# A gated linear-attention and adapter kernel: one decay array per chunk, work moved between engines, and an order written out by hand

## The chip, the cores and the metric

The kernel runs on one core of a Trainium2 chip. The time is device time in microseconds (us), from a launch of the whole program; "before" was run three times. The core has five engines that each work through their own queue in order: TensorE (PE in the profile; PEld is its weight load), VectorE (DVE), ScalarE (ACT), GpSimd (POOL) and SyncE (SP), which here only issues transfers. They meet through semaphores. SBUF is the working memory of 128 partitions; PSUM, in eight banks, receives TensorE's results.

## The reference

There are 4 batches, 8 heads, 768 tokens and 48 dimensions per head. Each head carries a 48 x 48 state:

```
cur   = (u * k_t) outer v_t
y_t   = r_t @ (state + cur)
state = w_t[:, None] * state + k_t outer v_t
```

The 8 heads of a token make a row x of 384. An adapter follows, with 8 experts of rank 16, of which the two with the largest logit are used:

```
logits = x @ w_gate
w      = softmax over the two largest logits
out    = x + sum over those two e of  w_e * (x @ A[e]) @ B[e]
```

## The kernel before

Tokens are cut into chunks of 128; 6 chunks make one batch's sequence, 24 chunks (t = 0 to 23) the whole. A tile of r and k (`rk`, loaded by SP into a ring of 10, 512 KB with padding at first, 384 KB in two transfers later) has the head dimensions of two heads on its 128 partitions, so 4 pairs x 128 tokens are 512 elements for r and as many for k.

Inside a chunk the recurrence is written as matrix products, with decays as exponentials of summed logarithms. For each chunk:

- `ln` (L174, ScalarE) takes the logarithm of w, two chunks at a time.
- `cs` (L186, L189, TensorE) sums it over tokens by a matmul with a triangle. The triangle is 256 wide: its first half gives the sum before a token, for r; its second half the negative sum up to a token, for k. The result `cs_ps` has 1,024 elements and fills two PSUM banks. Two chunks make a frame (FRAME = 2): in the second chunk of a frame, another matmul with `ones` (L189) adds the whole of the first.
- `exps` (L202, ScalarE) exponentiates all of it in place, and `mult` (L211, VectorE) multiplies r and k by it in one instruction: `rkd`.
- `amm` (L255, TensorE) multiplies the decayed k by the decayed r, per head: scores `a_ps` in two banks. `aev` (L261, VectorE) masks them: `at`.
- `qmul` (L206, GpSimd) is r times k; `dgmm` (L229, TensorE) sums it with u: 8 numbers per token. `dgev` (L241, VectorE) copies these out of PSUM, and `dv` (L246, GpSimd) multiplies v by them.
- `ktr` (L224, TensorE) transposes k, `ktev` (L236, VectorE) copies it to `ks`, and `kv` (L271, TensorE) adds k outer v to the state `s_ps`, which lives in PSUM. `resc` (L276, VectorE) multiplies the state by the frame's decay, once per frame (8 times); `sev` (L282, ScalarE) copies it to `sb`.
- `ymm` (L289, L296, L301, TensorE) adds three parts into `y_ps`: dv, the old state times r, and `at` times v. `yev` (L307, ScalarE) copies it to `xT`.

The adapter works on groups of three chunks (the last two groups have two and one). `zl` (L325, TensorE) makes logits and x @ A in `z_ps`; `top`, `gsel`, `gnorm` (VectorE), `gexp` (ScalarE), `gmul`, `gmul2` (GpSimd) make the weights; `zw` (L391, VectorE) multiplies them in; `zT` (L402, TensorE) transposes, `zTev` (L410, VectorE) copies. Per chunk then `dmm` (L418, L420, TensorE) makes x plus the adapter's part in `d_ps`, `oev` (L425, ScalarE) copies it to `res` and `store` (L429, SP) sends it out. `z_ps`, `zT_ps` and `d_ps` share the tag "m" and with it a single PSUM bank.

The eight banks: `cs_ps` 2, `a_ps` 2, `kd` (for `ktr` and `dgmm`) 1, `s_ps` 1, `y_ps` 1, "m" 1.

Order: every stage has a number in `OFFSET`; stage f of chunk t is put at t + OFFSET[f], and the instructions are issued in that order (a late stage of an adapter group is moved back by up to two chunks). As each engine works in order, this list sets what stands behind what in every queue, SP's loads and stores among them. `consts` (L152 to L162) loads u, then the adapter's two weight arrays, and casts each on GpSimd right after its load.

Of the kernel before, what the change touches and what calls it, by code (L numbers as in the profile page):

```python
# [18 lines left out]
L = 128  # L19
NC = S // L  # L20
# [6 lines left out]
FRAME = 2  # L27
# [3 lines left out]
OFFSET = dict(  # L31
    load_w=-9.0,
    load_rk=-8.5,
    load_v=-8.0,
    ln=-3.0,
    cs=-2.6,
    decay=-2.45,
    exps=-2.4,
    qmul=-2.2,
    mult=-1.9,  # L40
    dgmm=-1.3,
    dgev=-1.1,
    dv=-0.9,
    amm=-1.25,
    aev=-0.8,
    ktr=-1.2,
    ktev=-1.0,
    kv=-0.5,
    resc=-0.3,
    sev=-0.2,  # L50
    ymm=0.2,
    yev=0.5,
    zl=1.0,
    top=1.1,
    gexp=1.2,
    gsel=1.25,
    gmul=1.3,
    gnorm=1.4,
    gmul2=1.5,
    zw=1.6,  # L60
    zT=1.7,
    zTev=1.8,
    dmm=2.0,
    oev=2.2,
    store=2.4,
)
# [3 lines left out]
def tile_kernel(ctx: ExitStack, tc: tile.TileContext, rk, w, v, ublk, aw, bm, out):  # L70
# [82 lines left out]
    def consts(t):  # L153
        if t == 0:
            nc.sync.dma_start(out=ub_f, in_=ublk)
            nc.gpsimd.tensor_copy(out=ub, in_=ub_f)
        if t == 1:
            nc.sync.dma_start(out=aw_f, in_=aw)
            nc.gpsimd.tensor_copy(out=aw_b, in_=aw_f)
        if t == 2:  # L160
            nc.sync.dma_start(out=b_f, in_=bm)
            nc.gpsimd.tensor_copy(out=b_b, in_=b_f)  # L162

    def ln(t):
        w_in, i = wseq[t]
        if t < 2:
            n = 1
        elif t % FRAME == 0:
            n = FRAME
        else:  # L170
            return
        lw = lws[(t // FRAME) % NLW]
        o = t % FRAME
        nc.scalar.activation(out=lw[:, o:o + n, :, 0:D].rearrange("p c h d -> p (c h) d"),  # L174
                             in_=w_in[:, 0:n].rearrange("p c (h d) -> p (c h) d", h=H), func=ACT.Ln)

    def lwof(t, p):
        lw = lws[(t // FRAME) % NLW]
        return lw[:, t % FRAME, 2 * p:2 * p + 2, :].rearrange("p a b -> p (a b)")

    def cs(t):
        cs_ps = pp.tile([128, P, 2, L], F32, name="cs_ps")
        for p in range(P):
            o = cs_ps[:, p].rearrange("p a b -> p (a b)")
            odd = t % FRAME
            nc.tensor.matmul(o, lhsT=lwof(t, p), rhs=tri.rearrange("p a b -> p (a b)"),  # L186
                             start=(p % 2 == 0), stop=not odd, skip_group_check=True)
            if odd:
                nc.tensor.matmul(o, lhsT=lwof(t - 1, p), rhs=ones.rearrange("p a b -> p (a b)"),  # L189
                                 start=False, stop=True, skip_group_check=True)  # L190
        st[t]["cs"] = cs_ps

    def decay(t):
        c = t % NC
# [4 lines left out]

    def exps(t):  # L200
        c_ = st[t]["cs"].rearrange("p a s b -> p (a s b)")
        nc.scalar.activation(out=c_, in_=c_, func=ACT.Exp)  # L202
# [6 lines left out]
    def mult(t):  # L209
        rkd = wk.tile([128, 2, P, L], BF16, name="rkd", bufs=3)  # L210
        nc.vector.tensor_mul(rkd, st[t]["rk"], st[t]["cs"].rearrange("p a s b -> p s a b"))  # L211
        st[t]["rkd"] = rkd
# [6 lines left out]
    def ktr(t):  # L219
        if t % NC == NC - 1:  # L220
            return
        kT = bank(t)[:, 0:256].bitcast(BF16).rearrange("p (a b) -> p a b", a=P)
        for p in range(P):
            nc.tensor.transpose(kT[:, p, :], st[t]["rkd"][:, 1, p, :], ident)  # L224
# [6 lines left out]
    def ktev(t):  # L231
# [4 lines left out]
        nc.vector.tensor_copy(out=ks, in_=kT[:, :, 0:D])  # L236
        st[t]["ks"] = ks

    def dgev(t):
        dg = wk.tile([128, H, 1], F32, name="dg")  # L240
        nc.vector.tensor_copy(out=dg.rearrange("p a b -> p (a b)"), in_=st[t]["kd"][:, 256:256 + H])  # L241
        st[t]["dg"] = dg

    def dv(t):
        o = dvs[t % NDV]
        nc.gpsimd.tensor_mul(o[:, :, 0:D], vseq[t], st[t]["dg"].to_broadcast([128, H, D]))  # L246
        st[t]["dv"] = o

    def amm(t):
        rkd = st[t]["rkd"]  # L250
        a_ps = pp.tile([128, 2, P, L], F32, name="a_ps")
        for h in range(H):
            p, g = divmod(h, 2)
            s_ = slice(g * 64, g * 64 + D)
            nc.tensor.matmul(a_ps[:, g, p, :], lhsT=rkd[s_, 1, p, :], rhs=rkd[s_, 0, p, :],  # L255
                             start=True, stop=True)
        st[t]["a_ps"] = a_ps

    def aev(t):
        at = wk.tile([128, 2 * P, L], BF16, name="at")  # L260
        nc.vector.tensor_mul(at, st[t]["a_ps"].rearrange("s g p f -> s (g p) f"),  # L261
# [12 lines left out]
    def resc(t):  # L274
        if "dec" in st[t]:
            nc.vector.tensor_mul(s_ps, s_ps, st[t]["dec"].to_broadcast([128, P, D]))  # L276

    def sev(t):
        if t % NC == NC - 1:
            return  # L280
# [4 lines left out]
    def ymm(t):
        c = t % NC
        y_ps = pp.tile([128, P, L], F32, name="y_ps")
# [3 lines left out]
        if c > 0:  # L291
            sb = st[t - 1]["sb"]
            for h in range(H):
                p, g = divmod(h, 2)
                s_ = slice(g * 64, g * 64 + D)
                nc.tensor.matmul(y_ps[s_, p, :], lhsT=sb[s_, p, :], rhs=st[t]["rkd"][s_, 0, p, :],  # L296
                                 start=False, stop=False, skip_group_check=True)
        for h in range(H):
            p, g = divmod(h, 2)
            s_ = slice(g * 64, g * 64 + D)  # L300
            nc.tensor.matmul(y_ps[s_, p, :], lhsT=vseq[t][:, h, :], rhs=st[t]["at"][:, g * P + p, :],  # L301
                             start=False, stop=(h >= H - 2), skip_group_check=True)
        st[t]["y_ps"] = y_ps
# [6 lines left out]
    gate_at, lag = {}, {}  # L310
    s0 = 0
    for n in [NG] * ((NT - 3) // NG) + [2, 1]:
        gate_at[s0 + n - 1] = (s0, n)
# [4 lines left out]
    def zl(t):
        if t not in gate_at:
            return  # L320
        t0, n = gate_at[t]
        z_ps = pp.tile([128, NG, ER + E], F32, name="z_ps", tag="m")
# [108 lines left out]
    LATE = (dmm, oev, store)
    stages = (load_w, load_rk, load_v, ln, cs, decay, exps, qmul, mult, ktr, dgmm, ktev, dgev, dv, amm, aev, kv,
              resc, sev, ymm, yev, zl, top, gexp, gsel, gmul, gnorm, gmul2, zw, zT, zTev) + LATE
    order = [(-6.0 + t, -1, t, consts) for t in range(3)]
    for i, f in enumerate(stages):
        last = None
        for t in range(NT):
            pos = t + OFFSET[f.__name__]
            if f in LATE:
                pos += lag[t]  # L440
                pos = pos if last is None else max(pos, last + (1.0 if t < NT - 4 else 0.3))
                last = pos
            order.append((pos, i, t, f))
    order.sort(key=lambda o: o[:3])
# [47 lines left out]
```

## Time and profile before

| | us |
|---|---|
| median of 3 runs | 169.59 |
| lowest and highest | 169.42, 170.21 |
| the profiled execution's own time | 169.85 |
| its span, from the first to the last instruction | 168.1 |
| mean granted TensorE clock | 0.83 of full |

In the profile's rows, a timeline line gives start, duration, engine, line and operation, out<-in with the tile names, and in brackets how long the engine had been idle and what ended that. A row of the groups gives the count, then busy time and the mean ns of one, then the idle time just before. A row of the waits reads: who waited for whom, us in total, times, the longest. A row of the windows gives for a stretch the busy time of PE, PEld, DVE, ACT and POOL, then the granted clock, the share of the DMA engines and GB/s.

### The profile page before, as it was taken

What the parts mean: (1) busy time and instruction counts of PE and PEld (TensorE: products, weight loads), DVE (VectorE), ACT (ScalarE), POOL (GpSimd) and SP (SyncE); (2) the same over time, 40 slices, a digit from 0 to 9 for tenths busy, and PEclk for the clock granted to TensorE, in tenths of its full rate; (3) what the DMA queues carried; (4) which work ended last, traced back from release to release, by engine and by line L of the source; (5) the groups of instructions that cost most, each with busy time, mean ns of one, the idle gap of its engine ahead of it and who ended that gap; (6) DMA issues with size and microseconds to landing.
All of it is one profiled execution on the core that took longest, in us unless ns stands there. A gap on an engine that the chain in (4) does not pass through costs nothing.

```text
span 168.1 us, 3434 instructions
## 1 busy us (share of the span) xinstructions
PE 104.3 (62%) x1360; PEld 73.0 (43%) x1360; DVE 84.5 (50%) x187; ACT 67.3 (40%) x123; POOL 59.4 (35%) x86
## 2 busy tenths in 40 slices
PE   0420368999698098817980988279818883675441
PEld 0200245567476066715760566147605662453220
DVE  6200067665647708781677087816681778241210
ACT  4340022634447038623670386326802762141321
POOL 7002754441545314424453244234423442011000
PEclk9999999999959759996997599858985898585555
DMA  5999999910099337543993276011101110110212
GB/s 179 294 293 416 419 346 326 267 45 4 0 133 291 97 113 194 185 124 37 253 276 95 74 224 211 14 47 47 51 0 47 46 53 0 35 62 12 82 47 94
DMA packets 9727, 23.25 MB, mean 138 GB/s; under 512 B 1456, under 2 KB 5040, under 8 KB 9712
## 3 DMA queue, kind: packets, MB, share of 16 engines
q1 hardware_dynamic: 8992, 20.68, 38.2%
q0 software_dynamic: 720, 2.36, 8.1%
q8 instruction: 10, 0.16, 0.4%
q14 instruction: 5, 0.04, 0.1%
HBM read 20.68 MB, written 4.72 MB: 151 GB/s over the span
## 4 chain that ended last, share of the span: by engine, by line
PE 41%; DVE 35%; DMA 6%; issue 5%; ACT 4%; POOL 4%; SPq 2%; POOLq 0%; DVEq 0%; ACTq 0%
DVE rkd L211 14%; DVE at L261 9%; PE cs_ps L186 8%; DMA aw_f<-in_aw_dram 6%; PE a_ps L255 5%; PE cs_ps L189 4%; PE kd L224 4%; PE d_ps L418 4%; DVE ks L236 3%; PE y_ps L301 3%; DVE zw L391 3%; PE d_ps L420 2%; PE y_ps L289 2%; PE y_ps L296 2%; PE s_ps L271 2%
## 5 line engine op out<-in xcount | busy, mean ns | idle before, releaser
L246 POOL TENSOR_TENSOR dv<-v_bf,dg 128x384 bf16<-128x384 bf16 x24 | 19.9, 829 | 56.6 <-DVE dg L241 47.6
L186 PE MATMUL cs_ps<-tri,lw 128*128 128x256 f16 x96 | 25.5, 342 | 13.9 <-DVE rkd L211 9.8
L202 ACT ACTIVATE cs_ps<-cs_ps 128x1024 f32<-128x1024 f32 x24 | 24.2, 1008 | 22.0 <-PE cs_ps L186 17.6
L211 DVE TENSOR_TENSOR rkd<-rk,cs_ps 128x1024 bf16<-128x1024 f32 x24 | 29.1, 1212 | 2.6 <-ACT cs_ps L202 2.3
L206 POOL TENSOR_TENSOR q<-rk 128x512 bf16<-128x512 f32 x24 | 30.4, 1265 | 0.0
L418 PE MATMUL d_ps<-ident,xT 128*128 128x96 bf16 x96 | 9.8, 238 | 32.5 <-DVE zw L391 31.2
L261 DVE TENSOR_TENSOR at<-a_ps,mask 128x1024 bf16<-128x1024 f32 x24 | 29.2, 1216 | 0.1
L425 ACT COPY res<-d_ps 128x384 f32<-128x384 f32 x24 | 11.5, 477 | 33.4 <-PE d_ps L420 33.4
L418 PEld LDWEIGHTS <-xT 128*128 128x128 bf16 x96 | 6.6, 111 | 36.1 <-DVE zw L391 32.7
L307 ACT CAST xT<-y_ps 128x512 bf16<-128x512 f32 x24 | 14.1, 587 | 14.5 <-PE y_ps L301 14.4
L241 DVE COPY dg<-kd 128x8 f32<-128x8 f32 x24 | 3.9, 164 | 30.3 <-PE kd L224 30.3
L186 PEld LDWEIGHTS <-lw 128*128 128x128 f16 x96 | 10.4, 115 | 17.2 <-ACT lw L174 6.2
L189 PE MATMUL cs_ps<-ones,lw 128*128 128x256 f16 x48 | 16.4, 358 | 0.0
L410 DVE COPY zT<-zT_ps 128x384 bf16<-128x384 bf16 (+2 forms) x9 | 3.0, 335 | 19.3 <-PE zT_ps L402 19.1
L229 PE MATMUL kd<-ub,q 128*128 128x8 bf16 x96 | 6.3, 172 | 10.2 <-POOL q L206 10.2
L301 PE MATMUL y_ps<-at,v_bf 128*48 128x128 bf16 x192 | 12.4, 267 | 0.0
L289 PE MATMUL y_ps<-ident,dv 128*128 128x128 bf16 x96 | 12.1, 265 | 0.0
L255 PE MATMUL a_ps<-rkd 48*128 48x128 bf16 x192 | 11.0, 244 | 0.6
L174 ACT ACTIVATE lw<-w_in 128x768 f16<-128x768 f32 (+1 forms) x13 | 10.3, 796 | 1.6 <-DMA w_in<-in_w_dram 1.5
L366 POOL TENSOR_TENSOR pe<-sel,ge 128x24 f32<-128x24 f32 (+2 forms) x9 | 2.1, 230 | 25.2 <-DVE sel L357 16.1
L276 DVE TENSOR_TENSOR s_ps<-s_ps,dec 128x192 f32<-128x192 f32 x8 | 2.9, 366 | 15.4 <-PE s_ps L271 15.4
L289 PEld LDWEIGHTS <-dv 128*128 128x128 bf16 x96 | 9.4, 122 | 2.0 <-issue 1.0
(47 smaller groups left out, 141.6 us busy)
## 6 DMA issues: line engine op xcount, KB each, us to landing
rk<-in_rk_dram SPq DMA_DIRECT2D x28, 192.0 KB, 4.9
rk<-in_rk_dram SPq DMA_DIRECT2D x10, 512.0 KB, 9.6
out_dram<-res SPq DMA_DIRECT2D x24, 192.0 KB, 1.9
w_in<-in_w_dram SPq DMA_DIRECT2D x11, 384.0 KB, 6.9
v_bf<-in_v_dram POOLq DMA_DIRECT2D x3, 576.0 KB, 6.7
v_bf<-in_v_dram POOLq DMA_DIRECT2D x1, 480.0 KB, 9.8
w_in<-in_w_dram SPq DMA_DIRECT2D x2, 192.0 KB, 3.6
aw_f<-in_aw_dram SPq DMA_DIRECT2D x1, 272.0 KB, 10.1
```

The source lines that it names most:

```text
L186: nc.tensor.matmul(o, lhsT=lwof(t, p), rhs=tri.rearrange("p a b -> p (a b)"), start=(p % 2 == 0), stop=not odd, skip_group_check=True)
L189: nc.tensor.matmul(o, lhsT=lwof(t - 1, p), rhs=ones.rearrange("p a b -> p (a b)"), start=False, stop=True, skip_group_check=True)
L202: nc.scalar.activation(out=c_, in_=c_, func=ACT.Exp)
L206: nc.gpsimd.tensor_mul(q, st[t]["rk"][:, 0], st[t]["rk"][:, 1])
L211: nc.vector.tensor_mul(rkd, st[t]["rk"], st[t]["cs"].rearrange("p a s b -> p s a b"))
L246: nc.gpsimd.tensor_mul(o[:, :, 0:D], vseq[t], st[t]["dg"].to_broadcast([128, H, D]))
L255: nc.tensor.matmul(a_ps[:, g, p, :], lhsT=rkd[s_, 1, p, :], rhs=rkd[s_, 0, p, :], start=True, stop=True)
L261: nc.vector.tensor_mul(at, st[t]["a_ps"].rearrange("s g p f -> s (g p) f"), mask.to_broadcast([128, H, L]))
L289: nc.tensor.matmul(y_ps[:, p, :], lhsT=st[t]["dv"][:, 2 * p:2 * p + 2, :].rearrange("p a b -> p (a b)"), rhs=ident, start=(p == 0), stop=F ...
L301: nc.tensor.matmul(y_ps[s_, p, :], lhsT=vseq[t][:, h, :], rhs=st[t]["at"][:, g * P + p, :], start=False, stop=(h >= H - 2), skip_group_che ...
L307: nc.scalar.copy(out=xT, in_=st[t]["y_ps"])
L418: nc.tensor.matmul(d_ps[:, p * 96:(p + 1) * 96], lhsT=st[t]["xT"][:, p, :], rhs=pick, start=(p == 0), stop=False, skip_group_check=True)
```

## The change

- **One decay array.** `cs` makes a single sum per chunk, with a 128-wide triangle, in one bank (`x_ps`, 512 elements). A frame is one chunk; the matmuls with `ones` are gone.
- **Two exponentials of it.** `expp` writes exp(+x) to SBUF, one column further right in rows of 129 (`ep`, three buffers, column 0 is 1), so that reading from column 0 gives the sum before a token. `expm` then writes exp(-x) over x in PSUM.
- **The product is split.** `rmul` (GpSimd) multiplies r by `ep`; `kmul` (VectorE) multiplies k by x.
- **Moved.** `ktev` goes from VectorE to ScalarE; `dv` from GpSimd to VectorE, where it reads the 8 numbers straight out of PSUM, and `dgev` is gone. `resc` now runs for every chunk that is not the last of a sequence, 20 times, with the last column of `ep`; the ScalarE step `decay` is gone.
- **Banks.** The freed bank goes to "m", which has two.
- **Order.** `OFFSET` is replaced by a list `ORDER` that names every stage and chunk. `ymm` is cut into `ymd`, `ymS` and `ymv`, the casts of `consts` into `castc`, so that each stands in the list by itself.

The core of the diff:

```
-FRAME = 2
+WL = 2
...
+load_w.0 load_rk.0 ln.0 cs.0 expp.0 expm.0 load_w.1 load_w.2 kmul.0 consts.0 ln.1 cs.1 expp.1 load_rk.1
+load_v.0 load_rk.2 load_v.1 rmul.0 amm.0 load_w.4 expm.1 aev.0 load_rk.3 kmul.1 qmul.0 ln.2 cs.2 expp.2
+expm.2 rmul.1 amm.1 aev.1 qmul.1 castc.0 dgmm.0 ktr.0 ktev.0 dv.0 kmul.2 kv.0 ymd.0 dgmm.1 ktr.1 cs.3 resc.0
+ymv.0 ktev.1 dv.1 sev.0 yev.0 expp.3 kv.1 expm.3 resc.1 sev.1 consts.1 load_rk.4 consts.2 load_w.6 rmul.2
...
+load_rk.9 qmul.4 dgmm.4 ktr.4 ktev.4 dv.4 ln.6 castc.2 castc.1 zl.2 top.2 gexp.2 gsel.2 ymd.3 ymS.3 ymv.3
...
+sev.10 ymd.10 ymS.10 ymv.10 yev.10 qmul.11 dgmm.11 load_rk.16 zw.8 zT.8 rmul.11 amm.11 ln.14 kmul.12 cs.13
+expp.13 expm.13 qmul.12 zTev.8 dmm.6 dmm.7 oev.7 store.7 rmul.12 dv.11 ymd.11 dgmm.12 ktr.12 ymS.11 ktev.12
+aev.11 ymv.11 amm.12 yev.11 load_rk.20 kmul.13 cs.14 expp.14 expm.14 dv.12 aev.12 oev.6 store.6 kv.12
+resc.12 sev.12 zl.11 top.11 gexp.11 gsel.11 ymd.12 ymv.12 yev.12 rmul.13 amm.13 qmul.13 dgmm.13 ktr.13
+ktev.13 qmul.14 load_rk.17 dmm.8 oev.8 store.8 kmul.14 cs.15 expp.15 expm.15 dv.13 ymd.13 dgmm.14 gmul.11
+gnorm.11 gmul2.11 ktr.14 ktev.14 ln.16 aev.13 kv.13 resc.13 sev.13 ymS.13 ymv.13 yev.13 rmul.14 amm.14
+kmul.15 cs.16 expp.16 expm.16 rmul.15 ln.18 zw.11 zT.11 dv.14 load_w.20 load_v.18 ymd.14 ymS.14 aev.14
+ymv.14 amm.15 yev.14 zTev.11 dmm.10 oev.10 store.10 kmul.16 cs.17 ln.20 aev.15 load_rk.18 qmul.15 dgmm.15
...
+ymv.22 yev.22 gmul.20 gnorm.20 gmul2.20 zw.20 zT.20 kmul.23 zTev.20 kv.22 resc.22 sev.22 rmul.23 amm.23
+aev.23 dmm.19 oev.19 store.19 dmm.18 oev.18 store.18 qmul.23 dgmm.23 dv.23 zl.22 top.22 gexp.22 gsel.22
+dmm.20 oev.20 store.20 ymd.23 ymS.23 ymv.23 yev.23 gmul.22 gnorm.22 gmul2.22 zw.22 zT.22 zTev.22 dmm.21
+dmm.22 oev.21 oev.22 store.21 store.22 zl.23 top.23 gexp.23 gsel.23 gmul.23 gnorm.23 gmul2.23 zw.23 zT.23
+zTev.23 dmm.23 oev.23 store.23
...
-        cs_ps = pp.tile([128, P, 2, L], F32, name="cs_ps")
...
+        x_ps = pp.tile([128, P, L], F32, name="x_ps")
         for p in range(P):
...
+            nc.tensor.matmul(x_ps[:, p, :], lhsT=lwof(t, p), rhs=tri, start=True, stop=True)
+        st[t]["x"] = x_ps
+
+    def expp(t):
+        ep = eps[t % NEP]
+        nc.scalar.activation(out=ep[:, :, 1:L + 1], in_=st[t]["x"], func=ACT.Exp)
+        st[t]["ep"] = ep
+
+    def expm(t):
+        x = st[t]["x"]
+        nc.scalar.activation(out=x, in_=x, func=ACT.Exp, scale=-1.0)
...
+    def rmul(t):
+        rd = wk.tile([128, P, L], BF16, name="rd", bufs=3)
+        nc.gpsimd.tensor_mul(rd, st[t]["rk"][:, 0], st[t]["ep"][:, :, 0:L])
+        st[t]["rd"] = rd
+
+    def kmul(t):
+        kd_ = wk.tile([128, P, L], BF16, name="kd_")
+        nc.vector.tensor_mul(kd_, st[t]["rk"][:, 1], st[t]["x"])
+        st[t]["kdec"] = kd_
...
-        nc.vector.tensor_copy(out=ks, in_=kT[:, :, 0:D])
+        nc.scalar.copy(out=ks, in_=kT[:, :, 0:D])
...
-        nc.gpsimd.tensor_mul(o[:, :, 0:D], vseq[t], st[t]["dg"].to_broadcast([128, H, D]))
+        dg = st[t]["kd"][:, 256:256 + H].rearrange("p (h o) -> p h o", o=1)
+        nc.vector.tensor_mul(o[:, :, 0:D], vseq[t], dg.to_broadcast([128, H, D]))
...
-        if "dec" in st[t]:
-            nc.vector.tensor_mul(s_ps, s_ps, st[t]["dec"].to_broadcast([128, P, D]))
+        if t % NC < NC - 1:
+            d_ = st[t]["ep"][:, :, L:L + 1]
+            nc.vector.tensor_mul(s_ps, s_ps, d_.to_broadcast([128, P, D]))
...
-        z_ps = pp.tile([128, NG, ER + E], F32, name="z_ps", tag="m")
+        z_ps = pp.tile([128, NG, ER + E], F32, name="z_ps", tag="m", bufs=2)
...
     with tc.manual_schedule(engines={ENG.PE, ENG.Activation, ENG.DVE, ENG.Pool, ENG.SP}):
-        for _, _, t, f in order:
-            f(t)
+        for o in ORDER.split():
+            f, t = o.split(".")
+            stages[f](int(t))
```

More of the change, by code (lines that the diff above doesn't have):

```diff
@@ L26 @@
 RING = 10
-FRAME = 2
+WL = 2
 NG = 3
[L31 to L66, printed above, removed]
+ORDER = """
@@ L153, in consts, with castc @@
     def consts(t):
[L154 to L162, printed above, removed]
+        f, d = ((ub_f, ublk), (aw_f, aw), (b_f, bm))[t]
+        nc.sync.dma_start(out=f, in_=d)
+    def castc(t):
+        f, o = ((ub_f, ub), (aw_f, aw_b), (b_f, b_b))[t]
+        nc.gpsimd.tensor_copy(out=o, in_=f)
     def ln(t):
@@ L290, in ymm, with ymS @@
                              rhs=ident, start=(p == 0), stop=False, skip_group_check=True)
[L291 to L297, printed above, removed]
+    def ymS(t):
+        if t % NC == 0:
+            return
         for h in range(H):
@@ L308, in yev @@
         st[t]["xT"] = xT
-    gate_at, lag = {}, {}
+    gate_at = {}
     s0 = 0
@@ L429, in store @@
         nc.sync.dma_start(out=out[t * 128:(t + 1) * 128, :], in_=st[t]["res"])
[L431 to L444, printed above, removed]
+    stages = (load_w, load_rk, load_v, consts, castc, ln, cs, expp, expm, qmul, rmul, kmul, ktr, dgmm, ktev, dv, amm,
+              aev, kv, resc, sev, ymd, ymS, ymv, yev, zl, top, gexp, gsel, gmul, gnorm, gmul2, zw, zT, zTev, dmm, oev,
+              store)
+    stages = {f.__name__: f for f in stages}
     with tc.manual_schedule(engines={ENG.PE, ENG.Activation, ENG.DVE, ENG.Pool, ENG.SP}):
-        for _, _, t, f in order:
-            f(t)
+        for o in ORDER.split():
+            f, t = o.split(".")
+            stages[f](int(t))
 def kernel(**inputs):
```

153 lines of the change are left out of this document (69 added, 84 removed).

## The prediction

> **What bounds the kernel now.** I read the page first (busy shares and the chain), then the timeline of the start, of one adapter group and of the end, then the waits, the windows and the price rows. The first rows say that no engine is full and that the chain hops between TensorE and VectorE.
>
> ```profile
> span 168.1 us, 3434 instructions
> ...
> PE 104.3 (62%) x1360; PEld 73.0 (43%) x1360; DVE 84.5 (50%) x187; ACT 67.3 (40%) x123; POOL 59.4 (35%) x86
> ...
> PE 41%; DVE 35%; DMA 6%; issue 5%; ACT 4%; POOL 4%; SPq 2%; POOLq 0%; DVEq 0%; ACTq 0%
> ```
>
> With every engine at 62% or less, the 168 us are waits, so I look for where all engines stand still. The timeline of the start shows the first such place:
>
> ```profile
> 6.18 1.22 DVE L211 TENSOR_TENSOR rkd<-rk,cs_ps 128x1024 bf16<-128x1024 f32 x1 [2.34 <-ACT cs_ps L202]
> ...
> 15.03 0.64 POOL L159 CAST aw_b<-aw_f 128x544 bf16<-128x544 f32 x1 [1.59 <-DMA aw_f<-in_aw_dram]
> ...
> 18.19 1.26 POOL L206 TENSOR_TENSOR q<-rk 128x512 bf16<-128x512 f32 x1
> ...
> 22.37 1.22 DVE L261 TENSOR_TENSOR at<-a_ps,mask 128x1024 bf16<-128x1024 f32 x1
> ```
>
> Chunk 0 is decayed at 6.18, but its mask product `at` starts at 22.37: the first q sits on GpSimd behind the casts of the adapter weights, whose transfers landed late. The second place comes once per adapter group of three chunks; the waits put a number on it, and the TensorE rows of one group show it (how long, in brackets, it sat idle):
>
> ```profile
> PE d_ps L418 <- DVE zw L391: 31.2, 8, 4.4
> ```
>
> ```profile
> 144.49 0.50 PE L418 MATMUL d_ps<-ident,xT 128*128 128x96 bf16 x4 [4.44 <-DVE zw L391]
> ...
> 145.10 0.63 PE L289 MATMUL y_ps<-ident,dv 128*128 128x128 bf16 x4
> ```
>
> z_ps and d_ps share one PSUM bank (tag "m"), so the d_ps matmuls wait until VectorE has read z_ps, and the recurrence's y_ps stands behind them on TensorE: 31.2 us in eight waits, 3.9 us each. Last, the end:
>
> ```profile
> 148.13 1.23 DVE L261 TENSOR_TENSOR at<-a_ps,mask 128x1024 bf16<-128x1024 f32 x1
> ...
> 157.60 0.61 PE L325 MATMUL z_ps<-aw_b,xT 128*128 128x136 bf16 x4 [0.38 <-DVE zT L410]
> ...
> 160.05 0.29 DVE L391 TENSOR_TENSOR zw<-z_ps,g 128x128 bf16<-128x128 f32 x1 [0.38 <-POOL g L383]
> ...
> 163.24 0.27 PE L402 MATMUL zT_ps<-ident,zw 128*128 128x128 bf16 x1 [0.61 <-ACT res L425]
> ...
> 164.70 0.48 ACT L425 COPY res<-d_ps 128x384 f32<-128x384 f32 x1 [1.51 <-PE d_ps L420]
> ```
>
> The last `at` (chunk 23) ends at 149.36. So the span is 23.6 us to the end of the first `at`, 125.8 for 23 more chunks (5.47 each) and 18.7 of tail. I forecast these three stretches anew.
>
> **The change part by part.** The price rows:
>
> ```profile
> L206 POOL TENSOR_TENSOR q<-rk 128x512 bf16<-128x512 f32 x24 | 30.4, 1265 | 0.0
> L261 DVE TENSOR_TENSOR at<-a_ps,mask 128x1024 bf16<-128x1024 f32 x24 | 29.2, 1216 | 0.1
> L211 DVE TENSOR_TENSOR rkd<-rk,cs_ps 128x1024 bf16<-128x1024 f32 x24 | 29.1, 1212 | 2.6 <-ACT cs_ps L202 2.3
> L186 PE MATMUL cs_ps<-tri,lw 128*128 128x256 f16 x96 | 25.5, 342 | 13.9 <-DVE rkd L211 9.8 <-ACT lw L174 4.1
> L202 ACT ACTIVATE cs_ps<-cs_ps 128x1024 f32<-128x1024 f32 x24 | 24.2, 1008 | 22.0 <-PE cs_ps L186 17.6 <-PE cs_ps L189 4.1
> L246 POOL TENSOR_TENSOR dv<-v_bf,dg 128x384 bf16<-128x384 bf16 x24 | 19.9, 829 | 56.6 <-DVE dg L241 47.6 <-DMA rk<-in_rk_dram 4.7 <-PE a_ps L255 4.3
> L189 PE MATMUL cs_ps<-ones,lw 128*128 128x256 f16 x48 | 16.4, 358 | 0.0
> L307 ACT CAST xT<-y_ps 128x512 bf16<-128x512 f32 x24 | 14.1, 587 | 14.5 <-PE y_ps L301 14.4
> ...
> L236 DVE COPY ks<-kd 128x384 bf16<-128x384 bf16 x20 | 6.9, 347 | 0.0
> ...
> L241 DVE COPY dg<-kd 128x8 f32<-128x8 f32 x24 | 3.9, 164 | 30.3 <-PE kd L224 30.3
> L391 DVE TENSOR_TENSOR zw<-z_ps,g 128x384 bf16<-128x384 f32 x7 | 3.9, 557 | 2.8 <-POOL g L383 2.8
> ...
> L276 DVE TENSOR_TENSOR s_ps<-s_ps,dec 128x192 f32<-128x192 f32 x8 | 2.9, 366 | 15.4 <-PE s_ps L271 15.4
> ```
>
> *Log sums.* 144 matmuls of 256 columns (25.5 + 16.4 = 41.9 us) become 96 of 128 columns: 36,864 columns become 12,288, a third, so about 14 us. TensorE falls from 104.3 to 76, 3.2 us per chunk.
>
> *Exponentials.* 24 of 1,024 elements become 24 + 24 of 512. Each lies between half of L202 (0.50) and L307 (0.59); I take 0.59 for the one into SBUF, 0.55 in PSUM. ScalarE also gets the 20 ks copies: 0.35 (VectorE's row) to 0.59, I take 0.48, between them. Its sum is 67.3 - 24.2 + 24 x 1.14 + 20 x 0.48 = 80, 3.3 per chunk.
>
> *VectorE.* It loses rkd (29.1), ks (6.9), dg (3.9) and the eight rescales (2.9). It gains k's product on 512 elements (between L391 and L211 on a line: 0.69, so 16.6), dv out of PSUM (as zw on 384: 0.56, so 13.4; at GpSimd's own price 0.83 it would be 20) and 20 rescales at 0.37 (7.3). 84.5 - 42.8 + 37.3 = 79, of which about 3 are memsets ahead of the work: 3.2 per chunk.
>
> *GpSimd.* It loses dv (19.9) and gains r's product, the shape of q but with rows 129 floats apart, which no row shows. Ends: q's 1.27, and twice that; I take 1.27, the same size and types: 59.4 - 19.9 + 30.4 = 70, 2.7 per chunk.
> The Trainium skill (GPSIMD Engine Reference, section 4.1 Engine selection) speaks against this edit: an elementwise multiply belongs on VectorE, GpSimd being about twice as slow with two inputs. The rows agree on the price (1.27 against 0.69). By that rule r stays on VectorE and the sum below is some 18 us more, its share going from 3.2 to 3.9 per chunk: here VectorE is the engine nearest to full.
>
> *The waits added.* x_ps is one bank: cs of chunk t+1 waits for kmul t, and what stands behind it on TensorE (kv, zl, the y of an older chunk) waits too. The loop is kmul 0.69, cs about 0.3 (an estimate from L186: four of half its columns, overlapping), exponentials 1.14: 2.2 us, under every engine's share, so it costs nothing while VectorE has an `at` and a dv (1.8) to do meanwhile; without that cover it shows in full, 1.5 us a chunk. The state is now rescaled every chunk: kv 0.3 (an estimate: eight matmuls, narrower than the scores' below), resc 0.37, a copy of about the same, a loop of 1.0, hidden likewise. dv (VectorE) and ks (ScalarE) now read one bank from two engines; if one must wait for the other it is at most 0.56, with the next `at` behind it on VectorE; I take half of one such wait in three chunks.
>
> *Two adapter banks, and the order.* d_ps of older chunks can now run while z_ps waits for its weights, and the order puts zT a chunk or more behind zl. One tie is left: in the order, zl.11 comes round to the bank of d_ps 6, whose copy oev.6 stands on ScalarE behind expm.14. I walked kmul.12 to kmul.16 by hand along the order with these prices and TensorE at the faster of its two paces (shown below). VectorE's starts: kmul.12 0, zT copy 0.7, dv.11 1.1, `at` 11 1.6, kmul.13 2.9, dv.12 3.6, `at` 12 4.1, rescale 5.3, done 5.7; idle until 6.8, since zl.11 starts only when oev.6 ends at 5.95; gate steps 6.8, kmul.14 7.7, dv.13 8.4, `at` 13 9.3, rescale 10.6, kmul.15 10.9, zw 11.6, dv.14 12.2, `at` 14 12.8, kmul.16 14.4. That is 3.6 per chunk, with one idle stretch of 1.1.
>
> So the period's floor is VectorE's and ScalarE's 3.2 to 3.3. How full an in-order engine gets is seen in these windows:
>
> ```profile
> 0.00:12.00 12.00, 2.90 (x12) 1.52 (x12) 4.01 (x10) 5.26 (x7) 3.13 (x14) 1.00 0.87 249
> 12.00:18.00 6.00, 0.00 (x0) 0.00 (x0) 0.00 (x0) 0.00 (x0) 1.13 (x3) 1.00 1.04 412
> 120.00:132.00 12.00, 7.51 (x94) 5.28 (x95) 5.77 (x15) 4.12 (x10) 2.89 (x5) 0.72 0.09 33
> 132.00:144.00 12.00, 7.07 (x124) 5.38 (x121) 9.42 (x21) 5.46 (x10) 5.39 (x7) 0.91 0.10 35
> ```
>
> VectorE (third busy column) reaches 9.42 of 12, 78%, in the best, part of an adapter wait included. At 78% the period is 4.1, by the walk 3.6; I take **3.85** per chunk.
>
> *Start.* The casts of the adapter weights go behind qmul.4 on GpSimd, and their two transfers behind rk3 and rk4 on SP's queue; nothing early needs them. Chunk 0: as now up to kmul near 6.2, `at` done near 8.5. Then transfers bind: ahead of rk1 and with it go w0, rk0, w1, w2, u (1.33 MB), itself 0.52, and up to 1.18 of v on GpSimd's queue: 3.0 MB at the first window's 249 GB/s is 12 us; with half of v, 9.8. I take kmul.1 at **11.6**. Later loads arrive at 412 GB/s, 0.9 MB in 2.2 us, ahead of the work.
>
> *Tail.* In the rows above, z_ps to the end of zw is 2.7 (157.60 to 160.34), which I take for the group of two as well; zT to the end of res is 1.9 (163.24 to 165.18), and the store 2.9 more (to 168.1). New, counted from the end of `at` 23: zl.22 at 0.1, zw done at 2.8, from there to res of chunk 21 again 1.9 and 0.3 more for a second zT (zl.23 takes the bank of that d_ps), so zl.23 at 5.0; then 2.7 + 1.9 + 2.9 and 0.1: **12.6** against 18.7.
>
> *Sum.* 11.6 + 22 x 3.85 (84.7) + 3.2 from kmul.23 to the end of its `at` (itself 0.69, a copy 0.35, a rescale 0.37, scores 0.6, `at` 1.22) + 12.6 = 112.1 of span. The profiled execution took 169.85 with a span of 168.1, so 1.75 lie around it: 113.85, and 0.26 off for the shown median 169.59: **113.6 us**.
>
> **The rivals.**
> *TensorE stays slow.* Eight score matmuls took two durations:
>
> ```profile
> 24.03 0.61 PE L255 MATMUL a_ps<-rkd 48*128 48x128 bf16 x8
> ```
>
> ```profile
> 63.39 0.40 PE L255 MATMUL a_ps<-rkd 48*128 48x128 bf16 x8
> ```
>
> A mean clock of 0.83 is two thirds full and a third half speed, so the 76 us would be 67 all fast and 101 all slow (1.5 times): 4.2 per chunk, which would be the bound. At 93% filled, the period is 4.5: 128 us. For it: a third of the columns' work is gone, so TensorE is less busy. Against: the windows' clock goes with the long stops (0.72 with two of them, 0.91 with part of one), and these go.
> The Trainium skill (TensorE: Matmul & The Clock Gate, Part 1: The HAM clock gate) lets the array run at half its clock until it was busy for about 3.4 us and again after an idle window of that length. By that rule the 4.4 us waits were just long enough to slow it, and without them it stays fast, which is the next rival; the first windows say 1.00 with nothing running, so this trace bears the rule out only later on.
>
> *TensorE fast throughout and VectorE nearly full.* Period 3.2: 99 us.
>
> *r's product costs twice q's on GpSimd.* Then GpSimd needs 3.96 per chunk and, 90% filled, sets 4.4: 126 us.
>
> *The adapter's wait stays*, since zT in the order still waits for zw: the change doesn't do what it says. Seven inner waits of 3.9 us come back: 27 more, 141 us. Against: in the order eight or more TensorE steps lie between zl and zT.
>
> *Slower: the loads come too late.* SP issues in order, and loads of rk now stand behind stores, which wait for res.
>
> ```profile
> rk<-in_rk_dram SPq DMA_DIRECT2D x28, 192.0 KB, 4.9
> ```
>
> If each of the 14 reloads (chunks 10 to 23) were issued only when its chunk is due, its 4.9 us would be bare each time: 69 more, 182 us. It decides from 4.0 us bare per load ((169.6 - 113.6) / 14). Against: in the order most stand one to four chunks ahead of their use; the nearest (rk18, rk23) two products ahead.
>
> **How the numbers follow.** Forecast (105 to 121) 0.54; TensorE slow 0.13; r's product dear 0.11; nearly full 0.11; adapter's wait stays 0.05; loads late 0.06, of which 0.05 is slower and 0.01 no change. Faster by over 0.5% (about what a measurement of this kernel can tell from no change) 0.94, within 0.01, slower 0.05. The range 103 to 134 leaves out most of "nearly full", the adapter's wait and the late loads.
>
> **What would show it.** The first `at` ends before 10 us; no TensorE wait on zw over 1 us between chunks 3 and 20; rd at 1.27 and kd_ at 0.69; VectorE the busiest, over 65% of the span; `at` to `at` 3.85 us; from the last `at` to the end under 13. Wrong would be: VectorE idle on rd or on rk's transfers, a granted clock near 0.5, or cs waiting for kmul while VectorE has nothing else.

## The result and the profile after

The kernel after takes 113.56 us (median of 4 executions, 112.86 to 113.86) against 169.5 before: a ratio of 0.669, 95% interval 0.665 to 0.673. The forecast was 113.6. A second set on another occasion gave 111.5 us and 0.664 (0.641 to 0.688); b1, b2 and b3 below ran beside that set. The profiled execution took 113.32 us with a span of 111.5, at a mean granted clock of 0.92.

The first fence is from the page of after, the second from the VectorE timeline, the third from the waits.

```profile
span 111.5 us, 3365 instructions
...
PE 80.7 (72%) x1312; PEld 60.1 (54%) x1312; DVE 77.0 (69%) x180; ACT 73.7 (66%) x159; POOL 66.7 (60%) x84
...
DMA 33%; DVE 22%; PE 21%; ACT 11%; issue 5%; SPq 3%; POOL 1%; POOLq 0%; ACTq 0%; DVEq 0%
```

```profile
8.40 1.23 DVE L265 TENSOR_TENSOR at<-a_ps,mask 128x1024 bf16<-128x1024 f32 x1 [1.97 <-PE a_ps L260]
11.98 0.69 DVE L221 TENSOR_TENSOR kd__166<-rk,x_ps 128x512 bf16<-128x512 f32 x1 [2.35 <-DMA rk<-in_rk_dram]
...
97.03 0.68 DVE L221 TENSOR_TENSOR kd__2160<-rk,x_ps 128x512 bf16<-128x512 f32 x1
...
98.20 1.23 DVE L265 TENSOR_TENSOR at<-a_ps,mask 128x1024 bf16<-128x1024 f32 x1
```

```profile
POOL g L371 <- DVE den L365: 14.5, 8, 3.8
POOL pe L358 <- ACT ge L345: 13.0, 6, 3.4
DVE dv L252 <- ACT ks L246: 11.2, 13, 1.7
...
PE zT_ps L386 <- DVE zw L377: 3.4, 3, 2.2
```

The three stretches can be read off the timeline. The first `at` ends at 9.63 instead of 23.6. From kmul of chunk 1 (11.98, idle before it until the tile of r and k landed) to kmul of chunk 23 (97.03) is 85.05 us, 3.87 per chunk. The last `at` ends at 99.43, and 12.1 us follow, instead of 18.7. TensorE's wait of 31.2 us for zw has shrunk to 3.4. What is left is spread thin: in the chain no compute engine has more than 22%, and the longest waits belong to GpSimd, for gate steps (TensorE's list has no wait for the r products that stand behind them). In their place there is one new wait on VectorE: dv for ks, 11.2 us in 13 pieces.

The prices, from the groups of after:

```profile
L216 POOL TENSOR_TENSOR rd<-rk,ep 128x512 bf16<-128x512 f32 x24 | 28.3, 1182 | 9.6 <-ACT ep L202 5.2 <-DMA rk<-in_rk_dram 4.3
...
L211 POOL TENSOR_TENSOR q<-rk 128x512 bf16<-128x512 f32 x24 | 30.4, 1273 | 0.4 <-POOL q L211 0.4
...
L202 ACT ACTIVATE ep<-x_ps 128x512 f32<-128x512 f32 x24 | 14.5, 604 | 9.0 <-PE x_ps L197 8.6
L207 ACT ACTIVATE x_ps<-x_ps 128x512 f32<-128x512 f32 x24 | 14.5, 603 | 0.0
...
L252 DVE TENSOR_TENSOR dv<-v_bf,kd 128x384 bf16<-128x384 bf16 x24 | 13.2, 552 | 11.4 <-ACT ks L246 11.2 <-PE kd L239 0.3
L197 PE MATMUL x_ps<-tri,lw 128*128 128x128 f16 x96 | 11.3, 252 | 17.0 <-ACT lw L187 6.5 <-DVE kd__166 L221 4.5 <-DVE kd__1583 L221 1.9
```

Some executions of a kernel take up to 6% longer than its fastest; the times below are medians of the others, two to four of them; of a1 there was only one, at 151.2 us, and its other three took 158 to 159.

### The profile page after: what moved, and what is told of

It reads as the page before. It is cut to its first block, busy times and chain, and to the rows that moved or that the text cites. A ratio compares the mean times of both kernels' runs of the same rounds, so it can differ in the third digit from the quotient of the medians.

```text
span 111.5 us, 3365 instructions
## 1 busy us (share of the span) xinstructions
PE 80.7 (72%) x1312; PEld 60.1 (54%) x1312; DVE 77.0 (69%) x180; ACT 73.7 (66%) x159; POOL 66.7 (60%) x84
## 3 DMA queue, kind: packets, MB, share of 16 engines
q0 software_dynamic: 720, 2.36, 12.6%
## 4 chain that ended last, share of the span: by engine, by line
DMA 33%; DVE 22%; PE 21%; ACT 11%; issue 5%; SPq 3%; POOL 1%; POOLq 0%; ACTq 0%; DVEq 0%
DMA rk<-in_rk_dram 29%; DVE at L265 6%; DMA out_dram<-res 4%; DVE dv L252 4%; PE d_ps L402 3%; ACT res L407 3%; ACT ks L246 3%; PE d_ps L400 3%; PE x_ps L197 2%; ACT x_ps L207 2%; PE y_ps L306 2%; DVE s_ps L281 2%; PE z_ps L325 2%; PE a_ps L260 2%; DVE zw L377 2%
## 5 line engine op out<-in xcount | busy, mean ns | idle before, releaser
L216 POOL TENSOR_TENSOR rd<-rk,ep 128x512 bf16<-128x512 f32 x24 | 28.3, 1182 | 9.6 <-ACT ep L202 5.2
L197 PE MATMUL x_ps<-tri,lw 128*128 128x128 f16 x96 | 11.3, 252 | 17.0 <-ACT lw L187 6.5
L252 DVE TENSOR_TENSOR dv<-v_bf,kd 128x384 bf16<-128x384 bf16 x24 | 13.2, 552 | 11.4 <-ACT ks L246 11.2
L202 ACT ACTIVATE ep<-x_ps 128x512 f32<-128x512 f32 x24 | 14.5, 604 | 9.0 <-PE x_ps L197 8.6
L207 ACT ACTIVATE x_ps<-x_ps 128x512 f32<-128x512 f32 x24 | 14.5, 603 | 0.0
L407 ACT COPY res<-d_ps 128x384 f32<-128x384 f32 x24 | 11.3, 489 | 4.6 <-PE d_ps L402 4.2
L246 ACT COPY ks<-kd 128x384 bf16<-128x384 bf16 x20 | 9.7, 486 | 3.5 <-PE kd L234 3.1
L371 POOL TENSOR_TENSOR g<-pe,den 128x24 f32<-128x24 f32 (+2 forms) x9 | 2.0, 223 | 16.4 <-DVE den L365 14.5
L286 ACT CAST sb<-s_ps 128x192 bf16<-128x192 f32 x20 | 6.5, 326 | 5.8 <-DVE s_ps L281 4.7
L402 PE MATMUL d_ps<-b_b,zT 128*128 128x384 bf16 x24 | 9.4, 392 | 0.4 <-DVE zT L392 0.2
L300 PE MATMUL y_ps<-rd,sb 48*48 48x128 bf16 x160 | 9.0, 238 | 0.0
L306 PEld LDWEIGHTS <-v_bf 128*48 128x48 bf16 x192 | 7.0, 112 | 3.4 <-issue 1.3
```

What stands on the lines that cost most here:

```text
L197: nc.tensor.matmul(x_ps[:, p, :], lhsT=lwof(t, p), rhs=tri, start=True, stop=True)
L202: nc.scalar.activation(out=ep[:, :, 1:L + 1], in_=st[t]["x"], func=ACT.Exp)
L207: nc.scalar.activation(out=x, in_=x, func=ACT.Exp, scale=-1.0)
L216: nc.gpsimd.tensor_mul(rd, st[t]["rk"][:, 0], st[t]["ep"][:, :, 0:L])
L246: nc.scalar.copy(out=ks, in_=kT[:, :, 0:D])
L252: nc.vector.tensor_mul(o[:, :, 0:D], vseq[t], dg.to_broadcast([128, H, D]))
```

## The experiments

**Theory.** Three separate things went: the start (casts ahead of the first q), TensorE's stop in every adapter group, and part of the work per chunk, with VectorE as the engine whose work then sets the period. Each run below takes one thing back or moves one; their costs are not parts of one sum. **Rivals.** The order alone did it, without the new bank and arithmetic; or the transfers bind (the chain gives DMA 33%); or TensorE or the links between engines, not VectorE, set the period.

### a1: before, d_ps ahead of zl

```
-    dmm=2.0,
+    dmm=1.9,
-    oev=2.2,
+    oev=1.95,
```

> Before, with two numbers of the order changed: dmm from 2.0 to 1.9 and oev from 2.2 to 1.95, so that the d_ps matmuls of older chunks stand ahead of zl in TensorE's queue and no longer between zl and zw. One adapter bank as before. If the 31.2 us of TensorE waiting for zw are a matter of the order alone, six or seven inner waits of 3.9 us go, less about 1 us each because zl now waits for a res copy: 145 to 155 us. If only a second bank can remove them: 165 or more.

Measured: 151.2 us, against 169.6 for the kernel before beside it. The TensorE groups of a1:

```profile
L418 PE MATMUL d_ps<-ident,xT 128*128 128x96 bf16 x96 | 9.7, 235 | 4.1 <-DVE zw L391 3.0 <-DVE zT L410 0.7
...
L402 PE MATMUL zT_ps<-ident,zw 128*128 128x128 bf16 x24 | 3.7, 271 | 14.6 <-DVE zw L391 13.3 <-ACT res L425 1.2
```

The 31.2 us of d_ps waiting for zw are down to 3.0 with no second bank, so that wait was a matter of the order. But 13.3 of it came back at the next matmul that needs zw, zT. Removing 28 us of a wait brought 18 us at most, and 11 if 158 is taken for a1.

### a2: before, casts late

```
-            nc.gpsimd.tensor_copy(out=aw_b, in_=aw_f)
...
+    order += [(-2.05, -1, 0, castc), (1.5, -1, 1, castc), (1.55, -1, 2, castc)]
```

> Before, with the three casts of consts moved in GpSimd's queue: u behind the first q, the adapter's two weight arrays to just ahead of their first use. Nothing else. If the casts hold the start, the first at moves from 22.4 us to about 15 (u lands at 13.2 and is still ahead of it) and the time falls by about 7 us to 162 or 163. If the transfers hold the start, the first at stays above 20 and the time stays above 168.

Measured: 164.47 us, ratio 0.969 (0.953 to 0.985), against 169.6 beside it. In the VectorE timeline of a2, the first `at`:

```profile
16.62 1.22 DVE L262 TENSOR_TENSOR at<-a_ps,mask 128x1024 bf16<-128x1024 f32 x1
```

It stands 5.75 us earlier than in the kernel before, the last `at` 5.0 earlier (143.12 against 148.13), and the time fell by 5.2, not by the 7 expected: nearly all that the start loses, the end loses. The interval is wide; the shift is read from one trace each.

### b4: both in before

The two edits of a1 and the edit of a2 together.

> Before, with d_ps ahead of zl and the casts late, together: the kernel before with only its order mended, no new bank, no new arithmetic. The two alone gave 12 to 19 us and 6 us less. If they add up: 146 to 152, and the remaining 35 to 40 us to the kernel after come from the decay arrays, the moves and the second bank. If the order were nearly all of it: below 130.

Measured: 152.21 us, ratio 0.903 (0.897 to 0.909), with all four executions within 1.6 us of each other. The kernel before, mended at these two places of its order, gains 16 us of the 56. The other 40 came with the rest of the change; other orders of the kernel before were not tried. Whether a1 and a2 add up can't be said: with 151 for a1 they don't, with 158 they do.

### a3: after, one adapter bank

```
-        z_ps = pp.tile([128, NG, ER + E], F32, name="z_ps", tag="m", bufs=2)
+        z_ps = pp.tile([128, NG, ER + E], F32, name="z_ps", tag="m")
...
-gexp.5 gsel.5 dmm.2 rmul.7 amm.7 oev.2 store.2
+dmm.2 oev.2 store.2 zl.5 top.5 gexp.5 gsel.5 rmul.7 amm.7
```

(the same move in the later groups, each res copy put right behind its d_ps, and `bufs=2` taken from zT_ps and d_ps too)

> After, with one bank for the adapter's tiles instead of two, and its order changed only so far that every res copy follows its d_ps and no d_ps stands between a zl and its zT. If the second bank carries the gain, 7 groups lose 3 to 4 us each: 135 or more. If the order carries it, each group loses only the waits for res copies, 1 to 2 us: 120 to 128. No change (113 to 115) would say that neither counts.

Measured: 134.7 us, ratio 0.797 (0.781 to 0.812). Its waits:

```profile
DVE tp L336 <- PE z_ps L324: 16.4, 8, 4.7
DVE dv L251 <- ACT ks L245: 15.1, 13, 2.0
ACT res L406 <- PE d_ps L401: 11.1, 11, 2.9
...
PE d_ps L399 <- ACT res L406: 9.2, 9, 3.1
...
PE z_ps L324 <- ACT res L406: 6.2, 7, 1.4
```

Taking the second bank away costs about 21 us in the kernel after, at the edge of what the first reading expected, and by another path: not the old stop at zw, but TensorE waiting for res copies (9.2 and 6.2), with VectorE waiting behind it for z_ps (16.4; 1.8 in after). TensorE's clock has a part in it: kmul of chunk 13 is only 1.3 us later than in after (58.39 against 57.14), and 16 us are lost in the ten chunks behind it, where the windows of a3 give a granted clock of 0.64, 0.64 and 0.50 (60 to 96 us, in steps of 12) and those of after 1.00, 0.72 and 1.00. How much of the 21 is waiting and how much the slower TensorE, no run separates.

### b3 and b1: the start of after

b3 puts the adapter's loads and casts back where they stood; b1 moves one load; the yardstick is the kernel after, unchanged. The places of b3's edit in the order, then b1's edit:

```
-load_w.2 kmul.0 consts.0 ln.1
+load_w.2 kmul.0 consts.0 consts.1 consts.2 ln.1
...
-load_v.1 rmul.0
+load_v.1 castc.1 castc.2 rmul.0
...
-sev.1 consts.1 load_rk.4 consts.2 load_w.6
+sev.1 load_rk.4 load_w.6
...
-ln.6 castc.2 castc.1 zl.2
+ln.6 zl.2
```

```
-load_v.0 load_rk.2 load_v.1 rmul.0 amm.0
+load_v.0 load_rk.2 rmul.0 load_v.1 amm.0
```

> After, unchanged, as the yardstick for the three kernels beside it: 112.5 to 115 us.

> After, with the adapter's two weight loads put right behind that of u and their casts ahead of the first r product on GpSimd, as they stood before. If the casts set the start, the first at moves from 8.4 us to about 17 and the time rises by 6 to 9 us, to 119 to 123. If the later work catches up because the loads of r and k bind anyway, it rises by 3 or less.

> After, with the load of v for chunks 1 to 5 (1 MB) issued behind the first r product on GpSimd, some 3 us later, and nothing else. If the transfers ahead of the second r and k tile hold the start, kmul of chunk 1 moves from 12.0 us to about 10 and the whole time falls by 1 to 2 us. If the rest of the loads only change places, kmul of chunk 1 moves and the total stays within 0.7 us.

Measured for the yardstick: 111.5 us (0.664). For b3: 115.84 us (0.690, 0.678 to 0.701), 4.3 above the yardstick. For b1: 111.01 (0.661, 0.653 to 0.669). The VectorE timelines of the yardstick, b3 and b1, in this order:

```profile
8.56 1.22 DVE L265 TENSOR_TENSOR at<-a_ps,mask 128x1024 bf16<-128x1024 f32 x1 [2.24 <-PE a_ps L260]
11.52 0.69 DVE L221 TENSOR_TENSOR kd__166<-rk,x_ps 128x512 bf16<-128x512 f32 x1 [1.73 <-DMA rk<-in_rk_dram]
...
95.22 0.68 DVE L221 TENSOR_TENSOR kd__2160<-rk,x_ps 128x512 bf16<-128x512 f32 x1
```

```profile
14.28 1.23 DVE L264 TENSOR_TENSOR at<-a_ps,mask 128x1024 bf16<-128x1024 f32 x1 [7.78 <-PE a_ps L259]
...
15.42 0.68 DVE L220 TENSOR_TENSOR kd__170<-rk,x_ps 128x512 bf16<-128x512 f32 x1
...
99.12 0.68 DVE L220 TENSOR_TENSOR kd__2160<-rk,x_ps 128x512 bf16<-128x512 f32 x1
```

```profile
10.54 0.68 DVE L220 TENSOR_TENSOR kd__166<-rk,x_ps 128x512 bf16<-128x512 f32 x1
```

In b3 the first `at` is 5.7 us late, at 14.3 instead of the 17 expected, and kmul of chunk 1 only 3.9 (15.42 against 11.52), since it had to wait for its transfer anyway. So my 6 to 9 was too much: it left out that the transfer covers part of it. From chunk 2 to chunk 19 the kmuls are 3.0 to 3.6 us late, and that of chunk 23 by 3.9 again; against the first profile of after it ends 2.1 late (99.12 against 97.03), so the shift at the end is known to about 2 us. It speaks against the rival that the transfers bind. The chain of after lays everything from 4.7 to 34.7 us on transfers of rk. But in the yardstick engines wait for these transfers only twice, both times for chunk 1 (1.7 us before its kmul, 4.0 before its r product); in b3, which is later, they never do, and the delay stays. So the transfers hold chunk 1 alone. b1 brings its kmul forward by 1.0 us; its median is 0.5 lower, within the 0.7 of its second reading and inside the yardstick's interval, so no gain is shown.

### a4: r's product on VectorE

```
-        nc.gpsimd.tensor_mul(rd, st[t]["rk"][:, 0], st[t]["ep"][:, :, 0:L])
+        nc.vector.tensor_mul(rd, st[t]["rk"][:, 0], st[t]["ep"][:, :, 0:L])
```

> After, with r's product on VectorE instead of GpSimd. 24 times 0.69 = 16.6 us more on VectorE, whose 77 us become 93.6. If VectorE sets the period, nearly all of it shows: 126 to 131. If the period is set by loops and waits between engines with VectorE free a fifth of the time, half or less shows: 114 to 121.

Measured: 136.1 us, ratio 0.806 (0.794 to 0.818): about 23 us more, above both readings. The page of a4, then its timeline at two places:

```profile
PE 88.9 (66%) x1312; PEld 65.0 (48%) x1312; DVE 96.6 (72%) x204; ACT 74.9 (56%) x159; POOL 42.3 (32%) x60
```

```profile
73.38 2.48 POOL L211 TENSOR_TENSOR q<-rk 128x512 bf16<-128x512 f32 x2
73.48 2.95 DVE L216 TENSOR_TENSOR rd<-rk,ep 128x512 bf16<-128x512 f32 x1
76.35 0.68 DVE L221 TENSOR_TENSOR kd__1381<-rk,x_ps 128x512 bf16<-128x512 f32 x1
...
76.95 0.68 DVE L216 TENSOR_TENSOR rd<-rk,ep 128x512 bf16<-128x512 f32 x1
```

```profile
34.16 2.94 POOL L211 TENSOR_TENSOR q<-rk 128x512 bf16<-128x512 f32 x2
34.80 1.17 DVE L216 TENSOR_TENSOR rd<-rk,ep 128x512 bf16<-128x512 f32 x1
```

rd, both of whose inputs lie in SBUF, takes 0.68 us alone (76.95), but 2.95 when it starts 0.1 us after GpSimd starts two q's: it ends 0.57 after they do (75.86 to 76.43). Starting 0.64 us into a q (34.80), it takes 1.17 and gets in between the two, which then take 2.94 together instead of 2.48. Of the 24, 17 took 0.68 or 0.69, six 0.88 to 1.26 and one 2.95; together 21.2 us instead of 16.6. kmul, with one input in PSUM, keeps 0.67 to 0.69 in this run. The Trainium skill (GPSIMD Engine Reference, section 1, Specifications) says that GpSimd shares its SBUF interfaces with VectorE, with contention when a VectorE instruction has two SBUF inputs; these rows agree, and show it as a wait for the GpSimd instruction that is running, once for two of them.

The longer products add 4.6 us, a fifth of the 23. VectorE's own work rose by 19.6 in all (77.0 to 96.6), TensorE waited 17.0 us for rd ahead of the scores, and its granted clock was 0.84 instead of 0.92. The order of the list was written for r on GpSimd; one written for r on VectorE was not tried. In this order, leaving r on GpSimd saved about 23 us, where the forecast, by the rule of the Trainium skill (GPSIMD Engine Reference, section 4.1), had put 18.

### b2 and c2: two copies on the other engine

b2 moves ks from ScalarE back to VectorE; c2 is b1 with the nine zT copies moved from VectorE to ScalarE.

```
-        nc.scalar.copy(out=ks, in_=kT[:, :, 0:D])
+        nc.vector.tensor_copy(out=ks, in_=kT[:, :, 0:D])
```

```
-        nc.vector.tensor_copy(out=zT_[:, 0:n], in_=st[t]["zT_ps"][:, 0:n])
+        nc.scalar.copy(out=zT_[:, 0:n], in_=st[t]["zT_ps"][:, 0:n])
```

> After, with the ks copy back on VectorE, so that both readers of the kd bank are on one engine: VectorE gets 20 x 0.35 = 7 us more, ScalarE 9.7 less, and the 11.2 us in which VectorE waits for ks go. If VectorE's own work sets the period, the time rises by 3 to 7 us. If the wait between the engines is the dearer part, it falls by 1 to 4 us.

> After, with the v load of chunks 1 to 5 behind the first r product (that alone gave about 1.4 us) and the nine zT copies moved from VectorE to ScalarE. If VectorE's work sets the period, 3.0 us less on it bring 2 us more: 108 to 110. If ScalarE (73 us busy) is as near to the limit: 111 to 113.

Measured: b2 117.4 us (0.699, 0.680 to 0.718), 5.9 more than the yardstick; c2 119.7 (0.711, 0.703 to 0.718), 8 to 9 more than b1, outside both of its readings. The pages of the yardstick and of b2:

```profile
PE 77.4 (71%) x1312; PEld 57.0 (52%) x1312; DVE 76.7 (70%) x180; ACT 73.1 (67%) x159; POOL 66.5 (61%) x84
```

```profile
PE 83.4 (71%) x1312; PEld 62.1 (53%) x1312; DVE 82.4 (70%) x200; ACT 66.7 (57%) x139; POOL 66.6 (57%) x84
```

b2 fits the theory: VectorE's 76.7 us became 82.4, 5.7 more, and all of it shows. c2 doesn't: VectorE lost work, ScalarE got 4.1 us more than in b1, and it is the dearest of the small moves. The waits of c2:

```profile
DVE dv L251 <- ACT ks L245: 18.3, 14, 3.3
...
PEld L401 <- ACT zT L391: 7.7, 8, 1.6
...
PE d_ps L401 <- ACT zT L391: 6.3, 7, 1.5
```

zT now stands in ScalarE's queue, d_ps waits for it (6.3) with every other matmul behind it, and ks comes later still: dv waits 18.3 us instead of 11 or so. A copy of about 0.5 us at such a place costs about 1 us on average (8 to 9 us for nine), very unevenly: held against b1, the steps from kmul to kmul lose between 0.9 and 3.7 us at six places and nothing at most others. The largest, from kmul of chunk 13 to that of chunk 14, begins with d_ps waiting 1.3 us for zT. The granted clock has fallen to 0.50 in both kernels before that; b1 is back at 1.00 by 56 us, c2 only after 62. So here a short wait of TensorE went with more than its length, as the matmuls behind it ran slower.

### c3 and c4: is it VectorE, is it TensorE

c3 leaves out half of the mask product (the odd heads' y uses the even heads' `at`); c4 issues each cs matmul twice.

```
-        at = wk.tile([128, 2, P, L], BF16, name="at")
-        nc.vector.tensor_mul(at.rearrange("s g p f -> s (g p) f"), st[t]["a_ps"].rearrange("s g p f -> s (g p) f"),
-                             mask.to_broadcast([128, H, L]))
+        at = wk.tile([128, P, L], BF16, name="at")
+        nc.vector.tensor_mul(at, st[t]["a_ps"][:, 0], mask.to_broadcast([128, P, L]))
```

```
+            for _ in range(2):
+                nc.tensor.matmul(x_ps[:, p, :], lhsT=lwof(t, p), rhs=tri, start=True, stop=True)
```

> After, with half of the mask product left out: at is made for the even heads only, and the odd heads' y uses the even heads' at. VectorE loses 24 x 0.53 = 12.7 us, no other engine changes. If VectorE alone sets the period: 9 to 12 us less, 100 to 104. If TensorE and ScalarE, each over 80% busy in the middle, are as near to the limit: 5 us less or fewer, 107 to 112.

> After, with every cs matmul issued twice into the same place (the second overwrites the first): TensorE gets 96 matmuls of 128 columns more, some 5 us at its faster pace and 10 at the slower. If TensorE sets the period, it costs 5 to 10 us: 117 to 122. If VectorE sets it, only what lengthens the loop from kmul to the next kmul shows, 0 to 3 us: 112 to 115.

Measured: c3 110.56 us (0.657, 0.653 to 0.661); c4 112.9 (0.670, 0.664 to 0.677). The pages of c3 and c4:

```profile
PE 78.9 (73%) x1312; PEld 58.5 (54%) x1312; DVE 65.7 (60%) x180; ACT 73.2 (67%) x159; POOL 66.6 (61%) x84
```

```profile
PE 83.4 (74%) x1408; PEld 64.1 (57%) x1408; DVE 77.6 (69%) x180; ACT 73.3 (65%) x159; POOL 66.5 (59%) x84
```

This is where the theory falls. VectorE was relieved of 11 us (76.7 to 65.7), and the time fell by 1 to 3 (against the yardstick and against the first set of after). TensorE got 6 us more (77.4 to 83.4, at the same clock of 0.95), and the time rose by 1.4 at most. Each result fits the reading that clears its engine: neither engine's sum alone sets the period. c4 tests a TensorE that stays fast; what a slow one costs, it does not say. In c3 part of the freed time turned into waits, as its row for dv shows (10.8 us in the yardstick):

```profile
DVE dv L252 <- ACT ks L246: 14.3, 13, 1.7
```

**What the runs say together.** Work taken from one engine gives little (c3), work added to a link that others wait for costs its length or more (a4, b2, c2). The period of 3.87 us is that of a chain which goes from engine to engine in the written order, with all four at 60 to 72%. In a3, a4 and c2 TensorE was slower too: a granted clock of 0.81, 0.84 and 0.87 against 0.92 in after, and 88.5, 88.9 and 82.6 us for the 1,312 matmuls that took 80.7; what that adds is not separated from the waits. Which links carry the most is not settled here; ks on ScalarE, the matmuls that wait for zT and the r product are three that do. And no run takes back the single decay array by itself: what it gives of the 40 us is not shown.

## Why the prediction was right, point by point

- **The sum.** Its four terms came out at 12.0 (11.6 predicted), 85.1 (84.7), 2.4 (3.2) and 12.1 (12.6): each is near, and the rest cancels. That the total misses by less than 0.1 us is luck.
- **Start.** kmul of chunk 1 at 11.98 (11.6), held by its transfer, as predicted. The first `at` was to be done near 8.5; it ran from 8.40 to 9.63, since its scores stood on TensorE behind cs of chunk 1, which started only at 7.14, when its logarithm was done. That cost nothing, as kmul of chunk 1 waits longer. a2 and b3 show that the casts held the start of before, and that most of a shift there reaches the end.
- **Tail.** 12.1 us against 12.6 predicted, by the steps named: zl of chunk 23 starts when the res copy of chunk 21 ends.
- **Prices.** kmul 0.68 (0.69), dv 0.55 (0.56), exponentials 0.60 (0.59 and 0.55), cs 11.3 us in all (14), r's product 1.18 (1.27, and the dear rival's 2.5 is out). ScalarE's sum was too high, 73.7 against 80; TensorE's too low, 80.7 against 76. Both added and took off rows as if they were busy time, but instructions overlap at their edges and the rows count that twice: in after they add up to 84.4 for ScalarE and 104.9 for TensorE. GpSimd's 70 us are 2.9 per chunk by the division, not 2.7; with it the dear rival would have been at 4.2.
- **Period.** The number was right, 3.87 against 3.85. The step behind it failed in part: "the period's floor is VectorE's and ScalarE's 3.2 to 3.3", and VectorE as "the engine nearest to full". TensorE was busier (80.7 against 77.0), so the sign that VectorE be the busiest did not come. c3 shows that VectorE's work does not hold the time up: with 11 us less of it the period is 3.76, against 3.80 in the yardstick. The walk was too long at its own place: kmul.12 to kmul.16 took 12.85 us instead of 14.4, and the idle stretch before the gate steps of zl.11 was not there; the time went at other places, such as the one below. 3.85 was a choice between 3.6 and 4.1, and that it hit is in part luck.
- **A wait that was priced too low.** dv behind ks was put at half of 0.56 in three chunks, 2 us in all; it was 11.2. The share taken from the best window of before left room for it, without naming it. b2 shows that moving ks to VectorE doesn't pay. The wait is part of the period: at its longest, kmul of chunk 17 stands behind dv, as the rows below show, and the next cs on TensorE behind kmul (74.31, in the last rows of this document).

```profile
72.84 0.55 DVE L252 TENSOR_TENSOR dv<-v_bf,kd 128x384 bf16<-128x384 bf16 x1 [1.73 <-ACT ks L246]
73.31 0.36 DVE L281 TENSOR_TENSOR s_ps<-s_ps,ep 128x192 f32<-128x192 f32 x1
73.58 0.68 DVE L221 TENSOR_TENSOR kd__1583<-rk,x_ps 128x512 bf16<-128x512 f32 x1
```

- **Two banks.** The stop was rightly read, but not that the order alone can remove most of it (a1, b4). With the order of after, going back to one bank costs 21 us (a3).
- **Rivals.** TensorE stayed fast in most windows (mean 0.92), and c4 shows that its work at that pace is not the bound; the adapter's wait is 3.4 instead of 31.2; only chunk 1 waited for its load, 2.4 us on VectorE.

## What to carry to other kernels

Look first for places where all engines stand still, and ask whether a number in the order removes them before adding a buffer: here two numbers took 28 us of a wait away, though 18 at most of the time. Forecast a pipelined kernel in stretches (start, period, tail), and the period by a walk along the queues; a sum by engine says what is busy, not what sets the time, and taking work off the engine that is held to be the bound is the test. Busy time is less than the sum of an engine's rows, so do not add rows to it. A copy of 0.5 us can cost 1 us if it is put in a queue where others wait for it (c2).

## What the runs showed of the hardware that was not expected

- A VectorE product with both inputs in SBUF waited for GpSimd's running product: 0.68 us alone, 1.17 when it came 0.64 us into a q, 2.95 beside two q's (a4).
- On GpSimd, r's product with rows 129 floats apart was faster than q of the same size and types: 1.18 against 1.27 us in after (24 each).
- TensorE was slow behind a stop of 1.92 us, in the timeline of after: the same four cs matmuls took 0.39 before it and 0.58 behind it, and the granted clock was 0.50 from 75 to 80 us.

```profile
67.94 0.39 PE L197 MATMUL x_ps<-tri,lw 128*128 128x128 f16 x4
...
74.31 0.58 PE L197 MATMUL x_ps<-tri,lw 128*128 128x128 f16 x4 [1.92 <-DVE kd__1583 L221]
```

The prediction had read the Trainium skill (TensorE: Matmul & The Clock Gate, Part 1) as asking for an idle window of about 3.4 us; this stop was shorter, so one must not count on short stops being free.
